# One kernel, two fixed orders: a state-space layer and a long convolution on one core, with the scan's downward pass, the coarse scan and the turning of x cut differently

## The chip, the cores and the metric

The kernel runs on one core of one Trainium2 chip. The metric is device time in microseconds (us) of one execution; lower is better. Five engines work side by side, each through its own instructions in the order in which they were written: TensorE (PE: matmuls, with weight loads as PEld), VectorE (DVE), ScalarE (ACT), GpSimd (POOL) and SyncE (SP). SP, ACT and POOL also issue DMAs. An instruction starts when all before it on its engine have started or ended as the engine demands, and when the semaphores that it waits for are up.

## The reference

Two heads over a sequence of 2048 steps and 640 channels, all in bf16, side by side in the output.

Head A is a diagonal state-space layer with 640 complex states:

```
dt = exp(log_dt);  Lam_bar = exp(dt * Lam)
B_bar = ((Lam_bar - 1) / Lam)[:, None] * Bmat
Bu = einsum("bld,pd->blp", x, B_bar)
h_t = Lam_bar * h_{t-1} + Bu_t                 # 2048 steps
y = 2 * einsum("blp,dp->bld", h, Cmat).real + x * Dskip
```

Head B is a long convolution by channel, gated:

```
k_shift = four taps of k by shift_k            # causal, per channel
kv = k_shift * v
y = irfft(rfft(pad(kv)) * rfft(pad(ssm_k)))[:2048] + kv * ssm_D
out = q * y
```

## The kernel before

Head A. The 640 complex states stand as ten state tiles j = 0 to 9 of 128 rows (64 real parts, 64 imaginary parts). The 2048 steps are cut in 16 residues modulo 16, in two halves hf of eight; each half has two groups b of four. `dn{b}_{j}_{hf}` (L633, ten matmuls of 512 columns) projects x on tile j, from `xT`, x turned so that channels are rows. The first half of `xT` is made on TensorE: two loads `xn0`, `xn1`, then `px` (L582, transposes against the identity into PSUM) and `ex` (the copies to SBUF, by ACT or DVE). The second half comes by eight DMA transposes `x1..` (L597). B's four quarters `B00`, `B01` (states 0 to 319) and `B10`, `B11` (320 to 639) come by DMA transpose too (L608). Then a scan in three levels: `e1`, `m1`, `e3` go up inside a half; `S`, `eS`, `jw`, `jcw`, `jsw`, `jaw`, `scan` and their `v` twins (a_coarse) scan the 128 coarse steps of a group of tiles in one chain of DVE operations; `d1`, `a1`, `d00` to `a02` (a_down) go down again, matmul by matmul (L721, L738) with a DVE addition after each (L727, L744). `ct` and `ect` build the output matrix, `py{part}_{r}{i}` (L788, L792) projects the states and adds x times Dskip, `ey` copies to SBUF and `st` stores.

Head B works in five blocks G of 128 channels. Its FFT is done by matmuls: `s1` (L912, 32 matmuls) and `s2` (L948, 16) turn the filter (`h`, loaded by `hst`, completed by `dtap`) and the gated input (`k`); `pP`, `pQ`, `pY` multiply spectra on DVE; `i2` (L1004, 16) starts the way back, `zt` (L1011) is a DMA transpose of 1 MB, `i1` (L1040, 64 matmuls) ends it, `ob` multiplies by q and stores. Before it, `cv`, `cs`, `ca`, `cm` do the four taps and the gate, `kvs` writes the block to DRAM and `kvl` loads it in another layout. `e1h`, `e1k`, `e2h`, `e2k`, `e3` followed by two digits are the copies from PSUM (L212 on ACT, L214 on DVE).

What sets the order: `ORDER`, a string of operation names written out by hand or by a search beforehand. `place` walks it and emits each operation on its engine (`/A` ACT, `/D` DVE, `/G` POOL, `/S` SP where there is a choice). So each engine's queue is that string, filtered. `place` also gives out buffers: six of 8 KB a partition, seven of 4 KB, two for `yo`, and four PSUM tiles of two banks that every matmul group of the kernel shares. A group of matmuls waits until the last reader of its PSUM tile is done. SP's queue in the string's order carries nearly all loads, transposes and stores.

In `build` the coarse scan runs for tiles 0 to 3 and then for 4 to 9 (`NF` is 4), and a_down takes tiles in pairs.

Of the kernel before, what the change touches and what calls it, by code (L numbers as in the profile page):

```python
# [9 lines left out]
ALU = mybir.AluOpType  # L10
# [13 lines left out]
NF = 4  # L24
PEC = ()
# [111 lines left out]
ld_ldt ld_lre J0 consts J1 nrow ld_lim zero E0 pidx B00 w0 c4 nrowf ci0 xn1 xn0 par E1 ld_dsk/G B01 p0 dtb bc Dm0 w1 p1 fi w2  # L137
nrho ph mk ci1 px10 rn px12 ex10/D px14 ld_sk/S R px00 v0 wi0 px02 trig kz0/D wm0 ex02/A k0 rc px04 ex12/A ss ex00/A set_2_0/D
set_1_0/G ex14/A Dm1/S set_3_0/D x100 set_8_0/G ex04/A dn1_4_0 x101 set_12_0/G sk Ct dn0_4_0 x110 set_4_0/G cs200/A scol
set_3_1/D hst0/S set_1_1/G x111 dn0_1_0 e1_4_0/A set_2_1/G set_4_1/D dn1_1_0 cv300/A m1_4_0 set_12_1/G dn1_0_0 e1_1_0/D x120  # L140
e3_4_0/A ca200 dn1_2_0 ws0 x121 dn0_3_0 cs100/D ca100 x130 dn0_2_0 cs000/D dn1_3_0 x131 ca000 dn0_0_0 e1_3_0/A k1 cm00 m1_1_0
e1_0_0/A m1_3_0 kvs0/G dtap0/D e1_2_0/D m1_0_0 e3_1_0/A s1h03 e3_3_0/D B10 m1_2_0 s1h01 e1h03/D e1h01/A s1h00 e3_2_0/D
e3_0_0/D s1h02 e1h00/A kz1/D set_8_1/D dn0_3_1 e1h02/D B11 dn0_1_1 cs210/D wi1 s2h01 ct s2h00 dn1_3_1 wm1 dn1_1_1 e2h01/A
cv310/D kz2/G k2 k3 hst1/G e2h00/A dn0_2_1 dn1_2_1 e1_3_1/A e1_1_1/D dn0_0_1 ca210 e1_2_1/A dn1_0_1 cs110/D m1_3_1 ca110
e1_0_1/A m1_1_1 m1_2_1 m1_0_1 e3_3_1/D cs010/A e3_2_1/D dn1_9_0 e3_0_1/D e3_1_1/D S0 den v1 dtap1/G ca010 dn0_9_0 eS0/A jw0
ws1 jcw0 dn1_9_1 jsw0 jaw00 dn0_7_1 scan0 dn0_7_0 jcv0 dn1_7_1 kvl0/S e1_9_0/D V cm10 dn1_7_0 e1_7_1/A m1_9_0 kvs1/G dn0_9_1
e1_7_0/D m1_7_1 e3_9_0/D s2h02 e1_9_1/A g m1_7_0 m1_9_1 e3_7_1/A s1k03 e3_7_0/A e3_9_1/A s1k01 e2h02/D e1k03/A s1k00 s1k02
e1k01/A set_G_0/D s2h03 set_G_1/D e1k02/A jv0 v2 jsv0 e1k00/A jav01 s1h11 jav00 s1h12 e2h03/A e1h11/D d1_0 e1h12/A cv320/D
s1h10 a1_0 s1h13 hst2/S dn0_6_0 e1h13/A e1h10/D d00_0 s2h13 cs220/D s2k02 a00_0 e2h13/A dn1_6_0 e2k02/A s2k03 ca220 d01_0
s2h12 e1_6_0/A e2k03/D dtap2/G e2h12/A m1_6_0 a01_0 s2h11 s2h10 e3_6_0/A e2h11/A d02_0 cs120/D e2h10/A s1h22 a02_0 s1h21 s1h23  # L150
e1h22/A ca120 s1h20 kvl1/S e1h21/A dn0_5_1 e1h20/D cs020/A dn1_5_1 diagD dn1_5_0 ca020 e1h23/A s2k00 s2k01 e2k00/D dn0_5_0
e2k01/A s1k12 cn00 cn10 cm20 s1k13 e1k12/A kvs2/S e1_5_1/D s1k11 e1k13/A e1_5_0/D m1_5_1 s1k10 e1k11/A e3_5_1/D m1_5_0 kz3/D
e1k10/A dn0_4_1 s2k10 pP00 pQ00 e3_5_0/A cs230/A s2k11 pP01 dn1_6_1 pQ01 e2k11/A dn1_4_1 e2k10/A dn0_6_1 pY01 dn0_8_1 e1_4_1/A
pY00 e1_6_1/A i202 cn01 cn11 dn1_8_1 e302/A pP10 hst4/S m1_6_1 i201 pQ10 e3_6_1/A m1_4_1 i203 e301/A pY10 q0/S i200 e3_4_1/A
dn0_8_0 e300/A e303/D kvl2/S dn1_8_0 e1_8_1/D ct00 e1_8_0/A m1_8_1 cv330/D dtap4/G ct01 m1_8_0 e3_8_1/A ect00/D ct10 ect01/A
e3_8_0/D ct11 ct20 ect10/A S4 ca230 ect20/A ect11/A ct21 eS4/D ct30 ct31 ect21/A jw4 jcw4 ect31/A d1_1 jsw4 ect30/A ct40
ect40/A jaw40 ct41 zt0 s1k23 scan4 ect41/A s1k20 s1k21 e1k23/A s1k22 e1k21/A jcv4 e1k22/A jv4 a1_1 e1k20/A jsv4 d00_1 s2k20
jav41 cs130/A s2k21 jav40 e2k20/D d1_4 e2k21/A d1_3 a1_4 d1_2 a1_3 i101 a1_2 i210 ob01 i211 e310/A v3 e311/A py0_33 a00_1
ca130 d00_3 d00_2 d00_4 a00_3 py1_33 a00_4 py0_31 ey_33/A a00_2 st_33/S py1_31 cs030/D ca030 s2k13 s2k12 ey_31/A d01_2 cm30
e2k13/A st_31/S py0_00 e2k12/A kvs3/S a01_2 d01_3 pP11 s2k23 s2k22 e2k23/A pQ11 py1_00 e2k22/A pY11 py0_30 kvl3/S ey_00/A  # L160
a01_3 hst3/G st_00/S i213 i212 e313/A k4 d02_3 py1_30 e312/A kz4/D a02_3 d01_1 s1k33 ey_30/A a01_1 s2h22 s1h42 e1k33/A s2h23
e2h22/D s2h21 e2h23/A dtap3/G e1h42/D s2h20 st_30/S e2h21/A s1k30 e2h20/D s1k31 s1k32 e1k30/A pP20 e1k32/A py0_01 pQ20 e1k31/A
py1_01 pY20 d01_4 d02_1 ey_01/A d02_2 a01_4 cv340/A st_01/S s1h40 s1h41 a02_2 e1h40/A s1h43 a02_1 e1h41/A d02_4 cs240/D i100
e1h43/A ca240 py0_32 cs140/A a02_4 s2h42 py1_32 ob00 e2h42/A ca140 s1h30 ob0/S s1h31 ey_32/A cs040/D s1h32 e1h30/A st_32/S
s1h33 ca040 e1h31/A py0_22 e1h32/A py1_22 e1h33/A pP21 v4 q2/S s2k30 pQ21 s2k31 ey_22/A e2k30/A s2h43 st_22/S py0_11 pY21
e2k31/A s2h31 e2h43/A cm40 s2h30 e2h31/A py1_11 kvs4/S e2h30/A s2h40 s2h41 ey_11/D e2h40/A i222 st_11/G i221 e322/A py0_10
e321/D e2h41/A kvl4/G s2h32 i220 e2h32/D i223 q4/G e320/A py1_10 e323/A s2k32 pP30 s2k33 ey_10/A pQ30 s2h33 e2k33/A st_10/S
py0_21 pY30 e2h33/A s1k41 zt2 s1k43 e1k41/A e2k32/D py1_21 e1k43/A s1k40 ey_21/A s1k42 e1k40/A py0_20 st_21/G e1k42/A py1_20
s2k40 pP31 pQ31 q3/S pY31 s2k41 ey_20/A e2k40/D e2k41/A st_20/S zt1 i231 py0_12 pP40 e331/A i230 s2k42 pQ40 e330/A s2k43
py1_12 e2k43/A pY40 e2k42/A i232 i233 pP41 i120 e332/A q1/S e333/A pQ41 py0_23 ey_12/A pY41 py1_23 st_12/S zt3 ob20 i110  # L170
ey_23/A i240 ob10 i242 i241 e342/A i243 e340/D e341/A i121 st_23/S e343/A py0_03 ob21 zt4 ob2/G py1_03 i130 ey_03/A i131
st_03/G ob30 py0_13 ob31 py1_13 ob3/S i111 ey_13/A i141 st_13/S ob11 i140 ob41 ob1/S py0_02 ob40 py1_02 ob4/S ey_02/A st_02/S
# [3 lines left out]
class Kernel:  # L176
# [386 lines left out]
    def a_loads(self):  # L563
# [4 lines left out]
        for b in range(2):  # L568
# [3 lines left out]
            for k in (0, 2, 4):  # L572
                w = min(2, 5 - k)
                pt = self.g.buf("P", f"px{b}{k}")

                def f(e, k=k, w=w, pt=pt, xa=xa):
                    for kk in range(w):
                        for r in range(2):
                            for q in range(2):
                                c = 128 * (5 * (2 * q + r) + k + kk)  # L580
                                o = 512 * kk + 256 * r + 128 * q
                                nc.tensor.matmul(self.P(pt)[:, 0, :].bitcast(bf16)[:, o:o + 128], lhsT=self.S8(xa)[:, c:c + 128],  # L582
                                                 rhs=self.ident[:], start=True, stop=True, is_transpose=True)
                op(f"px{b}{k}", {"PE": mm_cost(128, 4 * w)}, f, r=[f"xn{b}", "ident"], w=[f"px{b}{k}"], bufs=[pt, xa],
                   due=self.DUE["x0"] + 0.5 * k + 3.0 * b)
                op(f"ex{b}{k}", {"ACT": act_c(512 * w), "DVE": dve_tt(512 * w)}, lambda e, b=b, k=k, w=w, pt=pt: self.copy(
                    e, self.xT[:, k:k + w, 0, 2 * b:2 * b + 2, :].rearrange("p k r m -> p k (r m)"),
                    self.P(pt)[:, 0, :].bitcast(bf16)[:, 0:512 * w].rearrange("p (k n) -> p k n", k=w)),
                   r=[f"px{b}{k}"], a=[f"x0{b}"], bufs=[pt], port=False)
# [22 lines left out]
    def a_up(self):  # L612
# [3 lines left out]
        self.Sb = self.cw[2]  # L616
# [30 lines left out]
    def a_coarse(self, js, due):  # L647
# [6 lines left out]
        t1, t2, vv = (self.cw[i] for i in range(3))  # L654
        ps = self.g.buf("P", f"pS{nm}")

        def fS(e):
            P = self.P(ps)[:].rearrange("p a n -> p (a n)")
            for i, j in enumerate(js):
                for c, (lt, q) in enumerate(((self.ident, 4), (self.M[4][:, j, :], 3), (self.M[8][:, j, :], 2), (self.M[12][:, j, :], 1))):  # L660
                    nc.tensor.matmul(P[:, 128 * i:128 * i + 128], lhsT=lt[:] if c == 0 else lt, rhs=self.Qb[:, j, q, :],
                                     start=(c == 0), stop=(c == 3))
        op(f"S{nm}", {"PE": mm_cost(128, 4 * n)}, fS, r=[f"q_{j}" for j in js] + [f"M_{m}_{h}" for m in (4, 8, 12) for h in sorted({j // 5 for j in js})] + ["ident"],
           w=[f"pS{nm}"], bufs=[ps], due=due)
        self.evac(f"eS{nm}", N, lambda: flat(self.Sb[:, 0:n, :]), lambda: self.P(ps)[:].rearrange("p a n -> p (a n)")[:, 0:N],
                  r=[f"pS{nm}"], w=["cw3"], bufs=[ps])
        sk = ["cw3"]
# [38 lines left out]
    def a_down(self, j0, due):  # L706

# [3 lines left out]
        js = (j0, j0 + 1)  # L711
        hs = sorted({j // 5 for j in js})
        nm = j0 // 2
        pt = self.g.buf("P", f"pd{nm}")

        def f1(e):
            P = self.P(pt)
            for i, j in enumerate(js):
                rhs = self.Qb[:, j].rearrange("p q n -> p (q n)")
                for n, w in ((4, 384), (8, 256), (12, 128)):  # L720
                    nc.tensor.matmul(P[:, i, 384 - w:384], lhsT=M[n][:, j, :], rhs=rhs[:, 0:w], start=(n == 4), stop=(n == 12))  # L721
        op(f"d1_{nm}", {"PE": mm_cost(768, 2)}, f1, r=[f"Q0_{j}" for j in js] + [f"q_{j}" for j in js] + ["Qz"] + [f"M_{n}_{h}" for n in (4, 8, 12) for h in hs],
           w=[f"pd{nm}"], bufs=[pt], due=due)

        def f2(e):
            o = self.Qb[:, j0:j0 + 2, 1:4, :].rearrange("p j q n -> p j (q n)")
            v.tensor_tensor(out=o, in0=self.P(pt)[:, :, 0:384], in1=o, op=ALU.add)  # L727
# [450 lines left out]
```

## Time and profile before

| | |
|---|---|
| median of three runs | 225.51 us (225.41 to 225.54) |
| profiled execution: its time | 225.54 us |
| profiled execution: span, first to last instruction | 223.7 us |
| PE busy | 191.3 us, 86%, 3942 matmuls |
| DVE busy | 176.6 us, 79%, 255 instructions |
| ACT busy | 143.5 us, 64%, 164 instructions |
| POOL busy | 30.2 us, 14% |
| DMA | 33.72 MB in 100454 packets, mean 151 GB/s |
| granted TensorE clock, mean | 0.988 |

The busy shares are averages. A matmul's recorded time runs on into the next one's, since matmuls are pipelined: 240 matmuls of L788 show 300 ns each, yet ten in a row take 1.47 us. So PE's work is better read from the distance between the starts of matmul groups. On DVE and ACT too a recorded time overlaps the next one a little: three copies of 1220 ns on DVE in a row take 3.48 us.

### The profile page before, as it was taken

Reading aid. Unit: us, or ns where it says so; the run is one execution under the profiler, and the core shown is the slowest. Engines: PE = TensorE matmul, PEld = TensorE weight load, DVE = VectorE, ACT = ScalarE, POOL = GpSimd, SP = SyncE. Lnnn points to the kernel's source line nnn. Section 1 sums busy time; section 2 is a strip of 40 time slices with the busy share of each in tenths; the row PEclk is TensorE's granted clock in tenths of the full one; section 3 lists DMA queues with packets and bytes.
Section 4 is the critical chain, followed back from the end, with each engine's and each line's share of the span. In section 5 each row is a group of like instructions: output and inputs, shape, how many; then the busy total and the mean of one; then the engine's idle time right before and its main releaser. Section 6 shows DMA issues by size and latency. Waiting matters only on the chain. (4 is left out here: it accounts for less than half of the span.)

```text
span 223.7 us, 8667 instructions
## 1 busy us (share of the span) xinstructions
PE 191.3 (86%) x3942; PEld 135.2 (60%) x3945; DVE 176.6 (79%) x255; ACT 143.5 (64%) x164; POOL 30.2 (14%) x41
## 2 busy tenths in 40 slices
PE   0077959999969998899979999989999999977792
PEld 0064536555555575555657776857878877875581
DVE  7589997788888799998899996999756948842460
ACT  3946935867385798687893176878887768561011
POOL 6619904000100000000000002000005010002100
PEclk9999996999999999999999999999999999999998
DMA  4998859974997059099192348700993999999576
GB/s 87 239 162 121 177 122 224 230 163 97 245 179 146 3 115 221 15 229 193 26 170 34 95 148 195 126 32 3 171 264 84 214 247 160 215 208 198 138 180 156
DMA packets 100454, 33.72 MB, mean 151 GB/s; under 512 B 96866, under 2 KB 98530, under 8 KB 100418
## 3 DMA queue, kind: packets, MB, share of 16 engines
q1 hardware_dynamic: 99204, 29.02, 67.8%
q0 software_dynamic: 1184, 4.16, 6.9%
q8 instruction: 30, 0.49, 1.0%
q14 instruction: 6, 0.05, 0.1%
q10 hardware_dynamic: 30, 0.00, 0.0%
HBM read 9.19 MB, written 7.86 MB: 76 GB/s over the span
## 5 line engine op out<-in xcount | busy, mean ns | idle before, releaser
L212 ACT CAST s<-ps 128x1024 bf16<-128x1024 f32 x82 | 78.9, 1022 | 23.4 <-PE ps L1004 8.2
L633 PE MATMUL ps<-xT,BC 128*64 128x512 bf16 x400 | 46.9, 381 | 2.1 <-ACT xT L212 0.9
L788 PE MATMUL ps<-BC,hb 128*128 128x320 bf16 x240 | 36.5, 300 | 0.0
L633 PEld LDWEIGHTS <-BC 128*64 128x64 bf16 x400 | 22.1, 110 | 21.3 <-issue 4.2
L212 ACT CAST yo<-ps 128x640 bf16<-128x640 f32 x15 | 10.4, 693 | 29.8 <-PE ps L792 23.0
L788 PEld LDWEIGHTS <-hb 128*128 128x128 bf16 x240 | 21.7, 98 | 11.8 <-issue 3.0
L912 PE MATMUL ps<-R,s 64*64 64x128 bf16 x1280 | 23.5, 224 | 6.1 <-DVE s L813 2.2
L214 DVE CAST s<-ps 128x1024 bf16<-128x1024 f32 x18 | 21.8, 1220 | 8.1 <-PE ps L948 4.2
L971 DVE TENSOR_TENSOR s<-s,s 128x2048 bf16<-128x2048 bf16 x20 | 24.4, 1223 | 3.1 <-DMA out_dram<-s 1.3
L912 PEld LDWEIGHTS <-s 64*64 64x64 bf16 x1280 | 20.2, 111 | 11.0 <-issue 8.0
L948 PE MATMUL ps<-s,Wre 128*64 128x128 bf16 x320 | 21.2, 222 | 0.8 <-ACT s L212 0.5
L1047 DVE TENSOR_TENSOR s<-ps,s 128x1024 bf16<-128x1024 f32 x10 | 12.0, 1221 | 12.4 <-PE ps L1040 12.4
L948 PE MATMUL ps<-s,Wim 128*64 128x128 bf16 x320 | 20.8, 219 | 0.0
L948 PEld LDWEIGHTS <-Wre 128*64 128x64 bf16 x320 | 17.9, 109 | 4.2 <-issue 2.2
L744 DVE TENSOR_TENSOR hb<-ps,hb 128x1024 bf16<-128x1024 f32 x15 | 18.0, 1220 | 2.1 <-PE ps L738 2.1
L879 ACT ACTIVATE s<-s,sk 128x2048 bf16<-128x2048 bf16 x8 | 16.1, 2016 | 4.6 <-DVE s L971 2.1
L887 DVE TENSOR_TENSOR s<-s,s 128x2048 bf16<-128x2048 bf16 x15 | 18.5, 1233 | 0.4
L948 PEld LDWEIGHTS <-Wim 128*64 128x64 bf16 x320 | 18.2, 110 | 0.3
L1040 PE MATMUL ps<-Ct,s 128*64 128x64 bf16 x640 | 11.8, 196 | 4.4 <-issue 4.3
L212 ACT CAST hb<-ps 128x768 bf16<-128x768 f32 x12 | 9.5, 800 | 9.2 <-PE ps L633 9.2
L971 DVE TENSOR_TENSOR s<-s 128x1024 bf16<-128x1024 bf16 x20 | 13.7, 688 | 0.3
L397 POOL TENSOR_TENSOR M<-E,ss 128x640 bf16<-128x640 bf16 x7 | 12.1, 1756 | 5.7 <-DVE ss L387 5.7
(159 smaller groups left out, 268.1 us busy)
## 6 DMA issues: line engine op xcount, KB each, us to landing
out_dram<-yo SPq DMA_DIRECT2D x13, 160.0 KB, 3.6
s<-kvd SPq DMA_DIRECT2D x4, 512.0 KB, 4.2
s<-in_B_q_dram SPq DMA_DIRECT2D x4, 512.0 KB, 5.3
out_dram<-s SPq DMA_DIRECT2D x4, 512.0 KB, 4.1
s<-in_B_ssm_k_dram SPq DMA_DIRECT2D x3, 512.0 KB, 5.0
kvd<-s SPq DMA_DIRECT2D x3, 512.0 KB, 3.4
s<-in_A_x_dram SPq DMA_DIRECT2D x2, 640.0 KB, 8.1
kvd<-s POOLq DMA_DIRECT2D x2, 512.0 KB, 5.7
```

Source lines behind the costliest of these rows:

```text
L212: self.nc.scalar.copy(out=out, in_=in_)
L214: self.eng[e].tensor_copy(out=out, in_=in_)
L397: self.eng[e].tensor_tensor(out=mt[:, js, :].rearrange("p j (r i) -> p j r i", r=2), in0=E[:].rearrange("p (a b i) -> p a b i", a=1, b=1). ...
L633: nc.tensor.matmul(P[64 * ri:64 * ri + 64, b, :], lhsT=self.BT[:, k, ri, 64 * j:64 * j + 64], rhs=self.xT[:, k, hf, 2 * b:2 * b + 2, :].re ...
L744: v.tensor_tensor(out=o, in0=self.P(p2)[:].rearrange("p j (h m) -> p j h m", h=2), in1=o, op=ALU.add)
L788: nc.tensor.matmul(P[:, part, 0:320], lhsT=hap(j), rhs=self.CT[:, j, c0:c0 + 320], start=(j == 0), stop=False)
L879: nc.scalar.activation(out=out, in_=k(j), func=ACT.Copy, scale=self.sk[:, G, j:j + 1])
L887: op(f"ca{j}{G}{h}", {"DVE": dve_tt(W_)}, lambda e, c=c, tt=tt: v.tensor_tensor(out=c(), in0=c(), in1=tt(), op=ALU.add), r=[f"tm{G}{h}"], ...
L912: nc.tensor.matmul(P[64 * ri:64 * ri + 64, r, 128 * b4:128 * b4 + 128], lhsT=d[64 * r:64 * r + 64, 4 * qd + b4, a0, :], rhs=self.R[64 * r: ...
L948: nc.tensor.matmul(P[64 * pi:64 * pi + 64, ri, 128 * k4:128 * k4 + 128], lhsT=W[:, kp, pi, :], rhs=A[:, kp + 16 * pi, :], start=True, stop ...
L971: v.tensor_tensor(out=o, in0=a, in1=b, op=op_)
L1047: v.tensor_tensor(out=o, in0=self.P(pt)[:].rearrange("p s (b a c) -> p a (s b) c", b=8, a=16), in1=o, op=ALU.mult)
```

## The change

`ORDER` is replaced by another string, and three parts of the work are cut differently; the arithmetic of the result is the same.

- x is turned with plain matmuls into f32 PSUM, one bank for each k (before: transposing matmuls into 16-bit PSUM, two k in one bank), and the copies `ex` read f32.
- a_down takes one tile at a time: ten `a1` of 384 columns and thirty `a0` of 512, each with matmuls of its own, in place of five `a1` of 768 and fifteen `a0` of 1024.
- The coarse scan runs for tiles 0 to 4 and 5 to 9, and its first copy `Sb` has a buffer of its own.

The string moves work between engines. ACT takes ten of the twenty scalings `cv`/`cs` (before eight), 13 of the unit copies `e1` (12), 12 of `e3` (10), 13 of `ey` (15); DVE takes the others. POOL builds eight of the twelve matrices `set` (before seven of twelve; two more, `set_G`, are on DVE in both). The head and the tail of the string, old and new:

```diff
 ORDER = """
-ld_ldt ld_lre J0 consts J1 nrow ld_lim zero E0 pidx B00 w0 c4 nrowf ci0 xn1 xn0 par E1 ld_dsk/G B01 p0 dtb bc Dm0 w1 p1 fi w2
-nrho ph mk ci1 px10 rn px12 ex10/D px14 ld_sk/S R px00 v0 wi0 px02 trig kz0/D wm0 ex02/A k0 rc px04 ex12/A ss ex00/A set_2_0/D
-set_1_0/G ex14/A Dm1/S set_3_0/D x100 set_8_0/G ex04/A dn1_4_0 x101 set_12_0/G sk Ct dn0_4_0 x110 set_4_0/G cs200/A scol
-set_3_1/D hst0/S set_1_1/G x111 dn0_1_0 e1_4_0/A set_2_1/G set_4_1/D dn1_1_0 cv300/A m1_4_0 set_12_1/G dn1_0_0 e1_1_0/D x120
-e3_4_0/A ca200 dn1_2_0 ws0 x121 dn0_3_0 cs100/D ca100 x130 dn0_2_0 cs000/D dn1_3_0 x131 ca000 dn0_0_0 e1_3_0/A k1 cm00 m1_1_0
-e1_0_0/A m1_3_0 kvs0/G dtap0/D e1_2_0/D m1_0_0 e3_1_0/A s1h03 e3_3_0/D B10 m1_2_0 s1h01 e1h03/D e1h01/A s1h00 e3_2_0/D
-e3_0_0/D s1h02 e1h00/A kz1/D set_8_1/D dn0_3_1 e1h02/D B11 dn0_1_1 cs210/D wi1 s2h01 ct s2h00 dn1_3_1 wm1 dn1_1_1 e2h01/A
...
-py1_12 e2k43/A pY40 e2k42/A i232 i233 pP41 i120 e332/A q1/S e333/A pQ41 py0_23 ey_12/A pY41 py1_23 st_12/S zt3 ob20 i110
-ey_23/A i240 ob10 i242 i241 e342/A i243 e340/D e341/A i121 st_23/S e343/A py0_03 ob21 zt4 ob2/G py1_03 i130 ey_03/A i131
-st_03/G ob30 py0_13 ob31 py1_13 ob3/S i111 ey_13/A i141 st_13/S ob11 i140 ob41 ob1/S py0_02 ob40 py1_02 ob4/S ey_02/A st_02/S
+xn1 ld_lre J0 consts nrow xn0 J1 zero ld_ldt E0 pidx w0 ld_lim c4 nrowf hst1/G B00 E1 kz0/G wi0 bc Dm0 px12 Dm1/G w1 px10
+ex12/A px14 ex10/A wm0 px00 w2 par px02 p0 ex00/D B01 px04 ex14/D dtb mk k0 R ex02/A p1 fi dtap1/G ex04/A s1h13 nrho ph rn Ct
+s1h10 ld_sk/S scol B10 e1h13/D s1h11 trig den dn1_4_0 e1h11/A rc B11 ss e1h10/A dn0_4_0 set_3_0/D set_1_0/G x100 dn0_1_0
+set_2_0/G e1_4_0/D x101 dn0_2_0 sk cs200/D set_8_0/G m1_4_0 v0 cv300/A dn1_2_0 kz1/G set_12_0/D set_3_1/G e3_4_0/A dn0_7_0
+e1_2_0/A set_1_1/G dn1_3_0 ca200 x110 set_2_1/G dn0_3_0 x111 cs100/A dn1_1_0 set_4_1/G x120 m1_2_0 set_4_0/D dn1_7_0 set_8_1/G
+x121 e1_1_0/A e1_3_0/A m1_1_0 ca100 x130 m1_3_0 e3_1_0/A dn0_0_0 e3_2_0/A e1_7_0/D cs000/A x131 dn1_0_0 set_12_1/D k1 g
+e3_3_0/A m1_7_0 s1h12 e1_0_0/A dn1_9_0 e1h12/A ca000 m1_0_0 dn0_9_0 ld_dsk/S cm00 dn1_6_0 e1_9_0/A kvs0/S e3_0_0/D dn0_0_1
+e3_7_0/D set_G_1/D dn1_0_1 set_G_0/D diagD dn0_1_1 dn1_1_1 e1_0_1/D kvl0/S hst0/S ws0 cs210/A wi1 m1_0_1 e1_1_1/D dn0_6_0 wm1
+m1_1_1 m1_9_0 e3_9_0/A ws1 v1 dn1_4_1 e3_1_1/D e3_0_1/D e1_6_0/D s1k03 s1k00 e1k03/D dn0_4_1 e1k00/D s1k01 dtap0/G V e1_4_1/A
...
+i232 st_23/S e333/A i230 pP41 i231 e332/A py0_33 pQ41 e330/A py1_33 pY41 e331/A zt3 py0_31 pP40 ey_33/A i243 pQ40 i242 e343/A
+py1_31 pY40 e342/A i241 ey_31/A st_33/S i240 e341/D i120 st_31/S e340/A i121 ob20 zt4 ob21 py0_11 i131 ob2/S py1_11 ob31 i130
+ey_11/A py0_22 st_11/S ob30 i141 ob3/S i140 ob41 py1_22 ob40 py0_20 ey_22/D ob4/S st_22/S py1_20 ey_20/A st_20/S
 """
...
-                                nc.tensor.matmul(self.P(pt)[:, 0, :].bitcast(bf16)[:, o:o + 128], lhsT=self.S8(xa)[:, c:c + 128],
-                                                 rhs=self.ident[:], start=True, stop=True, is_transpose=True)
+                                nc.tensor.matmul(self.P(pt)[:, kk, 256 * r + 128 * q:256 * r + 128 * q + 128], lhsT=self.S8(xa)[:, c:c + 128],
+                                                 rhs=self.ident[:], start=True, stop=True)
...
-        self.Sb = self.cw[2]
+        self.Sb = T([128, 5, 128], bf16, "Sb")
...
-    def a_down(self, j0, due):
+    def a_down(self, j, due):
...
+            rhs = self.Qb[:, j].rearrange("p q n -> p (q n)")
+            for n, w in ((4, 384), (8, 256), (12, 128)):
+                nc.tensor.matmul(P[:, 0, 384 - w:384], lhsT=M[n][:, j, :], rhs=rhs[:, 0:w], start=(n == 4), stop=(n == 12))
...
+            v.tensor_tensor(out=o, in0=self.P(pt)[:, 0, 0:384], in1=o, op=ALU.add)
...
+                src = self.Qb[:, j, 0:4, :].rearrange("p (h q) n -> p h (q n)", h=2) if r == 0 else hv(r - 1)
+                nc.tensor.matmul(self.P(p2)[:, 0, :].rearrange("p (h m) -> p h m", h=2), lhsT=M[1][:, j, :], rhs=src, start=True, stop=True)
...
+                v.tensor_tensor(out=hv(r), in0=self.P(p2)[:, 0, :].rearrange("p (h m) -> p h m", h=2), in1=hv(r), op=ALU.add)
...
-        self.a_coarse(list(range(NF)), U["c0"])
-        for j in range(0, NF, 2):
+        self.a_coarse(list(range(5)), U["c0"])
+        for j in range(5):
             self.a_down(j, U["d0"] + U["d1"] * j)
-        self.a_coarse(list(range(NF, 10)), U["c1"])
-        for j in range(NF, 10, 2):
-            self.a_down(j, U["e0"] + U["e1"] * (j - NF))
+        self.a_coarse(list(range(5, 10)), U["c1"])
+        for j in range(5, 10):
+            self.a_down(j, U["e0"] + U["e1"] * (j - 5))
```

## The prediction

> **What bounds the kernel now.** I read the totals first, then three long stretches of the span, then waits and groups, then the chain and the DMA queues. The stretches (busy us and, in brackets, instructions of PE, PEld, DVE, ACT, POOL) are cut where the string's work is comparable later on:
>
> ```profile
> span 223.7 us, 8667 instructions
> 0.00:48.80 48.80, 32.49 (x412) 20.73 (x414) 41.11 (x84) 31.51 (x39) 22.30 (x30) 0.97 0.92 175
> 48.80:148.60 99.80, 93.03 (x1872) 61.70 (x1874) 89.21 (x128) 69.41 (x81) 2.70 (x5) 1.00 0.64 125
> 148.60:223.70 75.10, 65.77 (x1665) 52.81 (x1664) 46.30 (x45) 42.62 (x46) 5.20 (x6) 0.99 0.81 169
> ```
>
> The reader is to see three regimes. Until 48.8 DMA is 92% busy and PE a third idle: loads set the pace. From 48.8 to 148.6 PE and DVE are both near full and neither alone is the bound. After 148.6 DVE has air and PE has none. The chain of waits says the same: from 150.5 on it is PE alone, matmul group after matmul group, but for two holes in which PE waits for nothing that the profile shows ("issue"):
>
> ```profile
> 198.90 1.17 PE ps L1040 x63
> 200.07 2.82 issue
> 202.89 0.19 PE ps L1040
> ...
> 206.19 1.73 PE ps L1040 x101
> 207.91 1.45 issue
> 209.36 0.60 PE ps L1040 x27
> ```
>
> Both holes lie inside one `i1` group, whose 64 matmuls have no wait between them. The DMA queues name a candidate:
>
> ```profile
> q8 instruction: 30, 0.49, 1.0%
> ```
>
> 30 packets of 16 KB for some 7,890 weight loads and matmuls are one packet for about 260 of them. Each hole ends 1.3 to 1.5 us after such a packet, and the two are 256 PE instructions apart. Where PE passes 256 instructions in normal time, they take 4.4 us and more; the ones ahead of these holes add up to 3.3 and 4.7 us of work, while a `zt` transpose of 1 MB fills the DMA engines. An inference, then: PE runs out of instructions.
>
> The other rows that the sum uses, as groups by shape and as waits:
>
> ```profile
> L744 DVE TENSOR_TENSOR hb<-ps,hb 128x1024 bf16<-128x1024 f32 x15 | 18.0, 1220 | 2.1 <-PE ps L738 2.1
> L727 DVE TENSOR_TENSOR Qb<-ps,Qb 128x768 bf16<-128x768 f32 x5 | 4.7, 952 | 0.7 <-PE ps L721 0.7
> L214 DVE CAST Qb<-ps 128x256 bf16<-128x256 f32 x10 | 3.9, 419 | 1.5 <-PE ps L641 1.5
> L683 DVE TENSOR_TENSOR cw<-sinT,ps 128x512 bf16<-128x512 bf16 x2 | 1.4, 688 | 1.5 <-PE ps L679 1.5
> L214 DVE COPY xT<-ps 128x1024 bf16<-128x1024 bf16 x1 | 0.7, 691 | 2.7 <-PE ps L582 2.7
> L397 POOL TENSOR_TENSOR M<-E,ss 128x640 bf16<-128x640 bf16 x7 | 12.1, 1756 | 5.7 <-DVE ss L387 5.7
> 34.23 2.63 SPq L608 DMA_TRANSPOSE BC<-in_A_B_re_dram  x1
> 36.91 3.10 SPq L608 DMA_TRANSPOSE BC<-in_A_B_im_dram  x1
> ```
>
> The last column of a group is DVE's idle time before it: fifteen paired additions L744 waited 2.1 us for PE together, 0.14 each.
>
> **The change part by part: the loads of the engines.** Downward pass on DVE: removed 15 x 1.220 + 5 x 0.952 = 23.1; added 30 x 0.688 (the row of 512 columns from PSUM) + 10 x 0.55 (between the rows of 256 and 512 columns) = 26.1, so +3.0. The copies of x on DVE: one of 0.691 becomes one of 1.220 and one of 0.688, +1.2. Changed choice of engine for copies, scalings and `set`: DVE -3.2, ACT +4.2 less 0.7 for x. Sum: DVE +1, ACT +3.5, PE unchanged but for two short `jw`, `jv` matmuls. No engine's total is a reason for a change of the time; the order is.
>
> I therefore added up, along both strings, each engine's durations ahead of given operations: on PE the usual distance between group starts (`dn` 1.1, `m1` 0.33, `s1` and `s2` 0.51, `i2` 0.5, `i1` 1.13, `py` 1.55), on DVE and ACT the rows' means. They are sums of queued work, not times. Before: when `dn1_9_0` starts at 48.76, PE has 28.6 us of work behind it, DVE 43.5, ACT 35.8; when `s1h40` starts at 148.59, 120.0, 138.7 and 110.4. After, ahead of `dn0_6_0`: 28.0, 39.0, 32.1; ahead of `d02_2`: 120.0, 134.6, 117.9.
>
> **First stage, to PE's 28 us of work: -3.4.** Before, PE is 20.1 us behind its work at its end. After:
> - `xn1`, `xn0` are issued at 0.74 and not at 3.11. They took 7.6 and 8.7 us to land, so `px` starts near 8.5 (before 10.74). But the small parameters now come later: `par` stands behind `px00`, so p0 is near 11 instead of 3.5; from there the DVE queue (ex00 1.2, ex14 0.7, mk and R 1.7, p1, fi, nrho 1.3), then rn 1.7 and trig 0.8 on ACT, rc and ss 1.3, give `ss` at 19.9 (before 15.7). Two `set` on POOL at 1.76 follow: `m1_4_0` near 23.5 (before 21.2), with 8.7 us of work ahead of it (before 7.1). So PE is 14.8 behind its work there, before 14.1: a small loss.
> - `B10`, `B11` (2.63 + 3.10 of SP) now stand ahead of all `x1`, with `k0` (2.9) and `ld_sk` (0.6) between. From B01's issue, which ended at 10.1 before and may end at 11.5 with `hst1`'s 0.5 MB on POOL's queue beside, B11 is issued out at 19 to 21 and lands 5.2 later (its row), at 24.5 to 26.5. `dn0_7_0` needs it near 25: at most 1.5 of wait.
> - That buys work of the first half for tiles 7, 9 and 6 while the `x1` transposes run. Before, PE had none left at 30.1 and stood 3 us. The eight `x1` (1.28 each when not held up), `v0` and the two B put the last issue at 33 to 37.5 and the landing, 1.7 to 3.3 later, at 35 to 41. `dn0_0_1` has 23.3 of work ahead: it starts at 38.2 at the earliest (14.9 behind), at 41 at the latest by these rows. I take 39.5, nearer the later bound since DMA was 92% busy, and 0.5 for copies: 16.7 behind, against 20.1.
>
> **Second stage, from 28 to 120: +1.6.** Before it took 99.8 us for 91.4 of PE and 95.2 of DVE. After: 92.0 and 95.6; I take the mean of the two additions, +0.5. ACT has 85.8 where it had 74.6; it stays below DVE, cost 0 as long as its two long blocks (`ws1` after `cs210`, `ct` of 4 us) lie where DVE empties PSUM, which the string does there. PE changes between kinds of group 92 times against 81; a change costs 0.13 (`s2` to `s2` 0.42, `s2` to `py` 0.57): 1.4, of which I take 0.5 since DVE shares the bound; ends 0 and 1.4. `kvl0` waits for `cm00` (near 38), `kvs0` (3.4 to 6.2 to land) and itself 4.2: 46.5 to 49 for `s1k03` wanted near 48: 0.6 taken, ends 0 and 2.5, `hst0` for `s1h02` behind it on SP included. The hand-overs from PE to DVE double to forty: a pair waited 0.14 on the mean, and the string puts other tiles' work between the steps of one tile, so I take 0 for the twenty more; ends -2 (the pairs' own 2.1 + 0.7 nearly gone) and +2.8 (twenty at 0.14).
>
> **Third stage, PE's last 64.5: +0.4.** PE work 64.7 against 64.5, changes 40 in both. For the instruction holes I added PE's work between every 256th instruction: near the end the new string has 4.28 and 3.59 with `zt3` and `zt4` under way; if each is stretched to the 6.2 us of the two stretched ones of before, that is 4.5 against 4.27. `zt4` (landing 7.2 to 8.5 after issue) has 9 us of other PE work between its last source `i240` and `i141`. Last copy and store are the same.
>
> The Trainium skill, page "Runtime: NRT & Kernel Launch", section "Instruction fetch mechanics", says that instructions come in 16 KiB blocks of 256 and that crossing a block is mostly hidden. The 2.82 and 1.45 us rows above speak against "hidden" here; by the page no string would lose time to fetch, the third stage's term would be 0 and the sum 223.7 us.
>
> **Sum.** 223.7 - 3.4 + 1.6 + 0.4 = 222.3 span. The profiled execution took 225.54 with 1.84 around its span, 0.03 above the median; so 224.1 us, 0.6% faster. A difference under about 0.2% (0.45 us) can't be told from none in this kernel.
>
> **Rivals.**
> - *Slower: the transposes are late.* One queue carries xn, B, k0, v0 and `x1`. If the last `x1` lands at 44 instead of 39.5 (hst1's 0.5 MB at 150 GB/s is 3.5 us more), PE stands as long: 228.6. It decides from a landing near 41. For it: DMA 92% busy. Against: the bytes ahead are the same but for hst1.
> - *Slower: single updates hand over badly.* Twenty more hand-overs through four PSUM tiles. At 0.14 each 226.9; at 0.5, the mean of the four that did wait for L738, 234. It decides from 0.07. Against: up to eight tiles are interleaved.
> - *Faster by more: no holes near the end.* The new tail puts a `py` group between nearly all `i1` groups. Without fetch holes 4.7 falls away: 219.4. Against: the sums of 3.59 and 4.28.
> - *No change:* the first stage's gain is returned in the second.
>
> **How the numbers follow.** Forecast, faster by 0.2 to 2%: 0.34. More than that: 0.16. Within 0.2%: 0.08. Late transposes: 0.20. Hand-overs: 0.22. So faster 0.50, same 0.08, slower 0.42. The range leaves out 1 in 10 at each end: from a little under the hole-free case, 217.5, to past the late transposes, 230.5. The forecast's own range is 221 to 225.
>
> **What the profile after would show.** First stage: `dn0_0_1` at 38 to 41, `ss` near 20, little PE wait between. Second: about 100 us from `dn0_6_0` to `d02_2`, a_down's additions on DVE idle little before they start. Third: issue holes of 4 to 5 us inside `i1` after `zt3`. Wrong if the first half's units wait for B11 beyond 27, if `s1k03` waits for `kvl0` by more than 3, or if DVE idles over 10 us in the second stage.

## The result, and the profile after

The changed kernel takes 218.79 us (median of 4 runs, 218.27 to 220.55) where before takes 225.52 (225.41 to 225.90). The ratio is 0.971, 95% interval 0.966 to 0.977: 2.9% faster. The forecast was 224.1 us and 0.6%, the range 217.5 to 230.5. On the two other chips that both kernels ran on, the ratio is 0.984 (0.977 to 0.991; before 223.64) and 0.974 (0.968 to 0.981; before 224.39). On the second of them four of six runs, 220.6 to 221.6 us, lie over 1.5% above the fastest and are not in the ratio; the median of all six, 220.9 us, is 0.984 of before. Single runs of the new kernel lie up to 4.3 us apart on one chip; part of that is explained below.

Here are the span of the profiled run (218.27 us in all) and the three stretches, cut at the same amounts of PE work as in the prediction (at `dn0_6_0` and `d02_2`). Columns as before: from and to, length, busy us and instructions of PE, PEld, DVE, ACT, POOL, then granted clock, DMA share, GB/s.

```profile
span 215.9 us, 8689 instructions
0.00:41.49 41.49, 32.27 (x382) 19.15 (x382) 36.51 (x95) 29.15 (x36) 20.71 (x29) 0.96 0.89 170
41.49:145.56 104.07, 97.30 (x2064) 66.06 (x2063) 91.28 (x124) 79.75 (x91) 7.94 (x10) 0.99 0.77 154
145.56:215.90 70.34, 65.42 (x1506) 51.61 (x1502) 49.77 (x51) 37.99 (x41) 2.58 (x3) 0.99 0.73 152
```

| stage | before | after | difference | predicted |
|---|---|---|---|---|
| first, to 28 us of PE work | 48.80 | 41.49 | -7.3 | -3.4 |
| second, to 120 | 99.80 | 104.07 | +4.3 | +1.6 |
| third | 75.10 | 70.34 | -4.8 | +0.4 |
| span | 223.7 | 215.9 | -7.8 | -1.4 |

The sum hides three larger misses: two stages gained more than forecast, one lost more. In the third stage the holes in which PE waited for nothing are gone. The chain of waits there is PE without a break, but for one copy on ACT and one wait for the transpose `zt4`:

```profile
191.31 1.00 PE ps L973 x32
...
193.91 1.02 PE ps L973 x32
194.95 1.02 ACT s L212
195.99 9.15 DMA s<-s
205.18 2.21 PE ps L1009 x128
```

The last line but one is `zt4`, 9.15 us from its issue until `i141` (L1009, the last line) starts; PE itself stood 1.0 us for it. The instruction queue moved as much as before. The groups that the prediction counted, with DVE's idle time in the last column:

```profile
q8 instruction: 30, 0.49, 1.0%
L735 DVE TENSOR_TENSOR hb<-ps,hb 128x512 bf16<-128x512 f32 x30 | 19.2, 684 | 5.6 <-PE ps L731 5.6
L721 DVE TENSOR_TENSOR Qb<-ps,Qb 128x384 bf16<-128x384 f32 x10 | 5.1, 551 | 0.1
L214 DVE CAST Qb<-ps 128x256 bf16<-128x256 f32 x8 | 3.2, 419 | 1.2 <-ACT s L212 0.7 <-PE ps L638 0.5
L397 POOL TENSOR_TENSOR M<-E,ss 128x640 bf16<-128x640 bf16 x8 | 14.5, 1845 | 3.9 <-DVE ss L387 3.9
14.32 1.55 SPq L605 DMA_TRANSPOSE BC<-in_A_B_re_dram  x1
15.91 2.98 SPq L605 DMA_TRANSPOSE BC<-in_A_B_im_dram  x1
```

The single additions cost what was forecast (0.684 and 0.551 us each), and DVE stood 5.6 us in front of them where it stood 2.1 in front of the pairs. `B10` and `B11` were issued by 18.9 us, earlier than the 19 to 21 reckoned with.

In the first stage `xn1` landed sooner than reckoned; the chain's line:

```profile
0.74 4.89 DMA s<-in_A_x_dram
```

In the second stage one wait is new. First the waits of the form that `dtap3` and `hst3` make, as totals of the whole run (us, times, longest; of the two on `PEld`, PE's weight loads, the one of 3.6 is that of `s1h13` at the start), then the rows around `s1h33`:

```profile
POOL s L803 <- DMA s<-in_B_ssm_k_dram: 12.6, 3, 6.4
PEld L881 <- POOL s L803: 5.7, 2, 3.6
```

```profile
140.20 0.24 PE L973 MATMUL ps<-s,Vim 64*128 64x128 bf16 x2
142.02 0.26 POOL L803 TENSOR_TENSOR s<-s,Dm 128x16 bf16<-128x16 bf16 x1 [6.37 <-DMA s<-in_B_ssm_k_dram]
142.33 3.30 PE L881 MATMUL ps<-R,s 64*64 64x128 bf16 x128 [1.90 <-POOL s L803]
```

`s1h33` (L881) waits for `dtap3` on POOL, and that for the load `hst3`, which POOL issued at 132.95 and which landed at 141.94. The last product ahead of it starts at 140.2, `s1h33` at 142.33: PE lost 2.1 us, 1.90 of it idle by the row. The expectations of `tap_later` and `half_tap` below say 2.7; that counts from 139.6, where `i221` starts, whose 16 products PE was still working on.

### The profile page after: what moved, and what is told of

Same layout as the page of the kernel before. It is cut to its first block, busy times and chain, and to the rows that moved or that the text cites. A ratio compares the mean times of both kernels' runs of the same rounds, so it can differ in the third digit from the quotient of the medians.

```text
span 215.9 us, 8689 instructions
## 1 busy us (share of the span) xinstructions
PE 195.0 (90%) x3947; PEld 136.8 (63%) x3947; DVE 177.6 (82%) x269; ACT 146.9 (68%) x166; POOL 31.2 (14%) x42
## 4 chain that ended last, share of the span: by engine, by line
PE 72%; ACT 7%; DVE 7%; DMA 7%; issue 4%; POOL 2%; ACTq 0%; POOLq 0%
PE ps L630 19%; PE ps L778 18%; PE ps L881 10%; PE ps L917 8%; DMA s<-s 4%; PE ps L973 4%; PE ps L1009 3%; PE ps L638 3%; ACT s L212 3%; DMA s<-in_A_x_dram 2%; DVE hb L735 2%; PE ps L782 2%; PE ps L715 2%; PE ps L731 2%; POOL M L397 1%
## 5 line engine op out<-in xcount | busy, mean ns | idle before, releaser
L630 PE MATMUL ps<-xT,BC 128*64 128x512 bf16 x400 | 46.4, 381 | 0.5 <-ACT Qb L212 0.5
L881 PE MATMUL ps<-R,s 64*64 64x128 bf16 x1280 | 25.0, 232 | 5.9 <-DVE Fi L337 3.5
L212 ACT CAST yo<-ps 128x640 bf16<-128x640 f32 x13 | 9.0, 691 | 28.5 <-PE ps L782 27.4
L881 PEld LDWEIGHTS <-s 64*64 64x64 bf16 x1280 | 21.4, 116 | 10.8 <-POOL s L803 5.7
L940 DVE TENSOR_TENSOR s<-s,s 128x2048 bf16<-128x2048 bf16 x20 | 24.4, 1221 | 0.7 <-ACT s L212 0.2
L735 DVE TENSOR_TENSOR hb<-ps,hb 128x512 bf16<-128x512 f32 x30 | 19.2, 684 | 5.6 <-PE ps L731 5.6
L848 ACT ACTIVATE s<-s,sk 128x2048 bf16<-128x2048 bf16 x10 | 20.0, 2013 | 3.7 <-DVE s L856 2.1
L917 PEld LDWEIGHTS <-Wre 128*64 128x64 bf16 x320 | 17.9, 109 | 4.7 <-issue 3.4
L856 DVE TENSOR_TENSOR s<-s,s 128x2048 bf16<-128x2048 bf16 x15 | 20.1, 1338 | 0.5 <-ACT s L848 0.3
L397 POOL TENSOR_TENSOR M<-E,ss 128x640 bf16<-128x640 bf16 x8 | 14.5, 1845 | 3.9 <-DVE ss L387 3.9
L212 ACT CAST hb<-ps 128x768 bf16<-128x768 f32 x13 | 10.3, 799 | 3.9 <-PE ps L630 3.8
L1009 PE MATMUL ps<-Ct,s 128*64 128x64 bf16 x640 | 11.5, 196 | 1.6 <-DMA s<-s 1.0
```

Of the source, the lines that this page charges most:

```text
L212: self.nc.scalar.copy(out=out, in_=in_)
L397: self.eng[e].tensor_tensor(out=mt[:, js, :].rearrange("p j (r i) -> p j r i", r=2), in0=E[:].rearrange("p (a b i) -> p a b i", a=1, b=1). ...
L630: nc.tensor.matmul(P[64 * ri:64 * ri + 64, b, :], lhsT=self.BT[:, k, ri, 64 * j:64 * j + 64], rhs=self.xT[:, k, hf, 2 * b:2 * b + 2, :].re ...
L735: v.tensor_tensor(out=hv(r), in0=self.P(p2)[:, 0, :].rearrange("p (h m) -> p h m", h=2), in1=hv(r), op=ALU.add)
L848: nc.scalar.activation(out=out, in_=k(j), func=ACT.Copy, scale=self.sk[:, G, j:j + 1])
L856: op(f"ca{j}{G}{h}", {"DVE": dve_tt(W_)}, lambda e, c=c, tt=tt: v.tensor_tensor(out=c(), in0=c(), in1=tt(), op=ALU.add), r=[f"tm{G}{h}"], ...
```

## The experiments

They ran in three sets, each on a chip of its own beside runs of before, which took 223.41, 223.64 and 224.39 us there. So ratios to before are compared, and times within a trace. In the second and third set the new kernel ran once more, unchanged.

**Are the holes at instruction numbers?** Before, with idle products put in where PE is idle anyway:

```diff
         op("par", {"PE": 0.1}, f_par, r=["praw", "ident"], w=["par"], bufs=[self.par], due=-25)
+        pad = self.g.buf("P", "pad")
+
+        def f_pad(e):
+            for c in range(64):
+                nc.tensor.matmul(self.P(pad)[:, 0, 0:10], lhsT=self.ident[:], rhs=self.ident[:, 0:10], start=True, stop=True)
+        op("pad", {"PE": 0.1}, f_pad, r=["ident"], w=["pad"], bufs=[pad])
```

> The kernel before with 64 idle 10-column products (128 PE instructions, weight load and matmul each) put on PE behind `par`, in its idle time before `px10` (2.9 to 10.7 us). Nothing else moves, but every 256-instruction boundary now falls 64 matmuls, one `i1` group, earlier in the work. Theory of instruction fetch (PE stands where a piece of 256 instructions holds less work than the fetch of the next one takes, about 3.5 us from boundary to boundary, 6.2 with a `zt` transpose on its way): the holes of 2.82 and 1.45 us inside `i121` and `i131` leave their places, and the ones of 1.57 and 1.2 at `s1h12` and `dn1_6_0` with them; new ones come where the shifted pieces are short, which at 61.4 (2.0 us of work), 76.9 (2.7), 140.4 (3.0) and 195.6 (3.3) they are; the time stays within -1 to +3 us of 225.5. Rival (the holes belong to the `i1` groups or to `zt`, not to instruction numbers): the holes stay at the same matmuls and the time is 225.5.

Measured: 1.016 of before (1.008 to 1.024), 226.2 us against 223.4. The holes inside `i121` and `i131` are gone, and those at `s1h12` and `dn1_6_0`. New ones lie inside `s2h03` (1.0 us), `s1h13` (0.9), `s1k31` (1.2), `py1_20` and `i111`. The last two in the chain of waits:

```profile
179.97 0.14 PE ps L799 x3
180.11 1.44 issue
181.55 1.52 PE ps L795 x10
...
207.58 0.30 PE ps L1047 x11
207.89 2.64 issue
210.53 3.38 PE ps L1047 x128
```

Counted by PE instructions all five stand where the four of before stood: at multiples of 256 behind one another, to within 6. Two of the four pieces named in advance ended in a hole (from 61.4, to `s2h03`, and from 140.4, to `s1k31`); at the ends of those from 76.9 and 195.6, with 2.7 and 3.3 us of work, there was no hole. The two largest holes, in `py1_20` and `i111`, were not named in advance: they end pieces with 4.8 us of work. So the holes do follow the instruction numbers, but a fixed price of 3.5 us for a piece is wrong both ways.

**Does the new order have no holes of itself?** The same 64 products in the new kernel, behind `px04`.

> The kernel after with the same 64 idle products, behind `px04`, where PE is idle from 10.1 to 13.6 us. Theory of instruction fetch: the boundaries leave the places they have now; pieces of 2.1 us (from 167.2) and 2.1 us (from 194.8) come up where PE has no slack, 1.4 us of hole at each, and some 0.9 more elsewhere in the last stage: +2 to +4 us over 218.8. Rival (the change got rid of the holes by putting other work between the `i1` groups): no holes, 218.8 within 0.5.

Measured: 1.008 of before (1.005 to 1.012), where the new kernel unchanged has 0.971 to 0.984 on three other chips: some 5 to 8 us lost with the order untouched. The holes inside groups lie in `s1h00`, `py0_30`, `i121` and `i130`, 1.5, 1.1, 0.8 and 2.5 us from one matmul to the next, each at a multiple of 256. The first and the last:

```profile
52.51 0.49 PE ps L888 x21
53.00 1.26 issue
54.26 0.36 PE ps L888 x11
...
206.27 0.69 PE ps L1016 x36
206.96 2.31 issue
209.28 0.75 PE ps L1016 x28
```

The rival has fallen. What keeps the new kernel free of such holes is where the boundaries lie in its string, not that `py` groups stand between `i1` groups. The loss is larger than forecast, among other things because the piece that ends in `i130` took 7.6 us and not the 6.2 assumed.

**Is the early B the gain of the first stage?** In the new order (the places that the units of tiles 7, 9 and 6 leave are not shown):

```diff
 scol
-B10
 e1h13/D
...
-B11
 ss
...
 x131
+B10 B11
 dn1_0_0
...
 m1_1_1
+dn0_7_0 dn1_7_0 e1_7_0/D m1_7_0 e3_1_1/D e3_0_1/D dn1_9_0 dn0_9_0 dn1_6_0
+e1_9_0/A e3_7_0/D dn0_6_0
 m1_9_0
...
+e1_6_0/D m1_6_0 e3_6_0/D
...
```

> The kernel after with `B10` and `B11` back behind all `x1` transposes, and the units 7, 9 and 6 of the first half, which need them, behind `dn1_1_1`. The prediction's reason for the first stage (work that needs no `x1` fills the time of the `x1` transposes): the fill is gone, but the `x1` are issued 4.5 us earlier, with a last landing near 29.5 where PE reaches `dn0_0_1` at 30.1; so PE still does not wait there, the two units' worth of order is worth nothing by itself, and the first 28 us of PE work end within 1 us of 41.5. Rival (the early B is the gain): PE stands 3 us or more near 30, as before, and the time is 3 to 5 us above 218.8.

Measured: 1.007 of before (1.004 to 1.011), so some 5 to 8 us above the new kernel by its ratios on three other chips. In PE's queue `dn1_4_1`, with 0.3 us more work ahead of it, starts at 52.21 and not at 43.5 to 44.9. PE's waits from 20 to 55 us (total, times, longest):

```profile
PE ps L638 <- DVE hb L214: 4.3, 4, 2.2
PE ps L638 <- ACT hb L212: 2.4, 3, 2.0
```

No wait is for `x1`, as the first theory said: `dn0_0_1` ran at 34.4 without one. But the time is lost all the same, the rival's 3 to 5 us or more: PE waits for copies of its own results, which stand on DVE and ACT behind the first group's convolution, `set_G` and `diagD`. Part of the longest wait is a load's: DVE itself stood 1.5 us in front of `diagD` for Dskip (`ld_dsk`). In the new kernel this window (18 to 50 us) has one wait:

```profile
PE ps L630 <- ACT Qb L212: 0.5, 1, 0.5
```

So the early B is a gain, and as these waits read it, by another mechanism than the prediction's: more tiles in flight give the copies time. The run moves `B10` and `B11` together with the units that need them and can't part the two.

**What was before's hole at 30 us?** In the order of before:

```diff
 cs100/D ca100
+dtap0/D
 x130
...
 kvs0/G
-dtap0/D
 e1_2_0/D
```

> The kernel before with `dtap0`, 0.2 us on DVE, moved up in DVE's queue from behind `cm00` to behind `ca100` (from 32.9 to about 29.7 us; its load landed at 27.9). The prediction took before's hole of 3 us at 30.1 for a want of work while the `x1` transposes run. Theory now (PE's order reaches `s1h03` there, and that waits for `dtap0` in DVE's queue): the wait of 2.2 us at 33.2 is gone, and the time falls by 1 to 2 us. The prediction's reason: PE meets the missing `x1` 2 us earlier instead, no gain.

Measured: 1.000 of before (0.997 to 1.004), no gain. `s1h03` starts at 29.58 and not at 32 to 33, but the next group, `m1_2_0`, then waits 2.45 us. PE's row, and what DVE did meanwhile:

```profile
32.68 0.49 PE L641 MATMUL ps<-hb,M 128*128 128x256 bf16 x3 [2.45 <-DVE hb L214]
```

```profile
28.48 0.75 DVE L881 TENSOR_SCALAR s<-s,sk 128x2048 bf16<-128x2048 bf16 x1
29.27 1.23 DVE L887 TENSOR_TENSOR s<-s,s 128x2048 bf16<-128x2048 bf16 x1
30.53 1.22 DVE L889 TENSOR_TENSOR s<-s,s 128x2048 bf16<-128x2048 bf16 x1
31.68 0.95 DVE L214 CAST hb<-ps 128x768 bf16<-128x768 f32 x1
```

The copy that `m1_2_0` needs (31.68) stands behind 3.2 us of convolution. Theory and rival both had this wrong: neither `dtap0` alone nor `x1` held PE, but DVE's queue.

**The 16-bit transposes of x.** The functions of before's `a_loads` in the new kernel (16-bit PSUM tile, `is_transpose=True`, copies of 16-bit columns); beside it the new kernel unchanged.

> The kernel after, unchanged, beside the runs of before that the next three are measured against: 0.971 of before (0.966 to 0.977) if the gain does not hang on the chip. On the chip of the first four experiments before took 223.4 and not 225.5 us; if after's gain lies in places that differ between chips, the ratio here moves towards 0.98, which is what the variant with the later `dtap3` gave there.

> The kernel after with the 16-bit transposes of x (transposing products into a 16-bit PSUM tile, and copies of 16-bit columns) of before put back; order and engines as in after. The prediction gave this part +1.2 us of DVE and +0.7 of ACT before 16 us, none of it named as bounding. If that is right, the time falls by 0 to 0.7 us. Rival (the copies set the start: `s1h13`, `ss` and with them `m1_4_0` stand behind them on DVE): `m1_4_0` moves from 20.8 to 19.6 and the time falls by 1.2 or more.

Measured: unchanged 0.984 (0.977 to 0.991), with 16 bit 0.990 (0.982 to 0.998). Its runs are 220.6, 220.9, 223.4 and 223.7 us, the unchanged kernel's 219.2 to 222.4. There is no gain, and in the profiled runs `m1_4_0` is later, at 24.3 and not 20.9 us. The reason is not the copies: two of them took 1.01 us on DVE (1.81 from 32 bits) and 1.93 on ACT in both forms. It is a load. The chain of waits of the 16-bit kernel's profiled run (223.4 us), and of the unchanged one:

```profile
5.12 11.11 DMA Dm<-in_B_ssm_D_dram
16.70 2.77 PE ps L884 x79
```

```profile
5.12 7.75 DMA Dm<-in_B_ssm_D_dram
13.44 2.78 PE ps L881 x92
```

`s1h13` waits for `dtap1` on POOL, and that for `Dm1`. Issued at 5.12 in both, it landed at 16.24 and at 12.88, and all that follows is 3.3 us later. From `s1h13` to the end the two traces take 204.3 and 203.9 us. So the 16-bit form is worth nothing either way that these runs can tell.

**What do single hand-overs cost in the old order?** Every `d1_k`, `a1_k`, `d0r_k`, `a0r_k` of before as two single ones, with the new kernel's `a_down`:

```diff
-d1_0
+d1_0 d1_1
...
-a1_0
+a1_0 a1_1
...
-for j in range(0, NF, 2):
+for j in range(NF):
```

> The kernel before with its downward pass one state tile at a time: every product and addition of a pair replaced by two single ones in its place (where no PSUM tile is free, behind the next copy that frees one), the coarse scan still of 4 and 6 tiles. DVE's work rises by 30 x 0.684 - 15 x 1.22 + 10 x 0.55 - 5 x 0.952 = 2.9 us, and hand-overs from PE to DVE double. Theory (the second stage was mis-sized by these hand-overs: after had 5.6 us of DVE idle in front of the single additions, before 2.1): the time rises by 3 to 6 us over before. Rival, the prediction's own 0 for the hand-overs: +1.5 at most, half of DVE's extra work.

Measured: 1.059 of before (1.053 to 1.064), 13 us, twice the theory's upper end. The groups:

```profile
L739 DVE TENSOR_TENSOR hb<-ps,hb 128x512 bf16<-128x512 f32 x30 | 19.2, 684 | 5.1 <-PE ps L735 4.9
L725 DVE TENSOR_TENSOR Qb<-ps,Qb 128x384 bf16<-128x384 f32 x10 | 5.5, 556 | 1.9 <-PE ps L719 1.8
```

Busy time rose by 2.0 and idle time in front by 4.2 over before's rows: 6.2 of the 13. The rest is spread over many short stops of PE around 112 to 147 us, each for an operation of ACT or DVE. The rival (+1.5) has fallen. How much of the 13 us belongs to the singles, and how much to an order never laid out for them, stays open.

**Moving the wait for `hst3`.** `d02_2`, `py0_12` and `py1_12` ahead of `s1h33` in the new order (the copy `ey_12` moves up with them; the places they leave are not shown):

```diff
 a02_8
+d02_2 py0_12
+a02_9 e321/A
+py1_12 a02_2
 s1h33
```

> The kernel after with `d02_2`, `py0_12` and `py1_12` put ahead of `s1h33`, which there waits 2.7 us for `dtap3` and the load `hst3` behind it (landed 141.94). Theory (the hole is PE's alone, and PE sets the end from there on): 2.2 to 2.7 us of the 2.72 are gained, 216.1 to 216.6. Rival (DVE, 0.88 busy in this stage, or the instruction pieces give it back): under 1 us gained.

Measured: 0.980 of before (0.975 to 0.985), 219.3 us, against 0.984 and 0.974 for the unchanged kernel in the other sets: not told apart. From `d02_9` to `s1k31` the trace takes 16.4 us, those of the unchanged kernel 17.0 to 17.2. The wait shrank, but a hole came at the next boundary, where 3.2 us of work were left for the piece:

```profile
149.22 1.01 PE ps L881 x47
150.23 1.14 issue
151.37 0.46 PE ps L881 x17
```

**A better version, in three steps,** with the unchanged kernel beside them. Only `d02_2` and `py0_12` moved (`half_tap`); then `Dm0` and `Dm1` moved ahead of `hst1`; then `py1_22` moved ahead of `i141`:

```diff
 J1
+Dm0
...
+Dm1/G
 hst1/G
...
 py0_22 st_11/S
+py1_22
 ob30 i141
```

> The kernel after, unchanged, as the measure for the three that follow: 0.971 of before on the first chip, 0.984 on the second; a value between these, its runs 219 to 221 us, some 2 to 3 us above where the small load `Dm1` lands late.

> The kernel after with `d02_2` and `py0_12`, but not `py1_12`, put ahead of `s1h33`. With both `py` moved, the wait of 2.7 us for `dtap3` was gone, but the piece of 256 instructions from `s1h32` to `s1k30` was left with 3.2 us of work, and a hole of 1.41 us came at its end. Theory of instruction fetch: here the piece keeps 4.5 us of work, no hole; 1.8 us of the wait are filled: 1.5 to 1.8 us below the unchanged kernel, against about 0.9 with both moved. Rival (the hole at `s1k30` has another cause): it stays, gain under 0.7.

> The last one, and the small load `Dm1` issued ahead of `hst1` on POOL's queue, near 2 us and not at 5.1. `dtap1` and, behind it on POOL, `ph` wait for it; it landed at 12.9 to 13.1 us in the short runs of after, and at 16.2 in the run of 223.4 us of the variant with 16-bit transposes, in which `s1h13` started at 16.7 and not at 13.4. Theory (this landing sets the start of PE's queue, and its spread is the spread of the runs): the runs above 221 us go, median 0 to 0.7 us lower. Rival (the spread is that of all loads in the first 16 us): same median and spread as the last one.

> The last one, and `py1_22` put ahead of `i141`, which waits 1.1 us for the transpose `zt4`. Theory of instruction fetch: the piece fetched while `zt4` is on its way comes 6.2 us after the last boundary whether PE waits for `zt4` or not, so the wait turns into a hole at the boundary: 0 to 0.3 us gained. Rival (the wait alone held PE): 1.1 us gained.

Measured: 0.974 (0.968 to 0.981) unchanged, 0.973 (0.969 to 0.978), 0.991 (0.987 to 0.994) and 0.984 (0.980 to 0.989).

The first step did what fetch theory says: no hole at `s1k30`, and 14.84 us from `d02_9` to `s1k31` (14.84 and 14.92 in the next two steps, which keep this order) where the unchanged kernel took 17.0 to 17.2 in all three of its traces. The times do not settle whether it is a faster kernel: the medians of all six runs are 218.7 and 220.9 us, but both spread too far. Five of its runs took 217.1 to 219.3 us; the profiled one took 221.9, with `Dm1` landing at 16.14.

The second step made it worse. `Dm1` lands no earlier than before, at 12.67 for an issue at 2.52, and `hst1`, now behind it, has become the last to come:

```profile
3.55 11.71 DMA s<-in_B_ssm_k_dram
15.73 2.78 PE ps L881 x84
```

`s1h13` starts at 15.7 in place of 13.4. Both sides were wrong: it is not `Dm1` that sets the start, but whichever of the two loads comes last. Nor is this start the whole of the spread: the profiled run of the unchanged kernel in this set took 221.2 us with `Dm1` landed at 12.83 and `s1h13` started at 13.5.

The third step shows the exchange that was forecast. The wait for `zt4` is gone, and a hole stands at the next boundary, inside `py0_20`:

```profile
209.04 1.46 PE ps L778 x10
210.51 1.71 issue
212.21 0.30 PE ps L782 x3
```

From `i131` to `py1_20` the two traces take 12.13 us without and 12.77 with the third step, as the theory has it. The times lean the other way (0.991 and 0.984, with intervals that overlap), so the exchange is shown and its price is not.

## Why the prediction was right or wrong

The sign and the range held. The sum was 5.3 us too high, 6.4 in the span (the new kernel's median lies 2.9 us above the profiled span, where 1.8 was reckoned), by the terms below. A gain of more than 2% had been given a chance of 0.16. The sign was partly luck: the stage that beat its forecast by most is one where a small loss was forecast, and 64 idle products ahead of it make the same order slower than before (1.008).

- **Third stage, +0.4, measured -4.8: the step that failed.** The prediction stretched the pieces of 4.28 and 3.59 us of work to 6.2 each, because before's two were stretched so: 4.5 us of holes, where none came. Stretching does not follow from `zt3` and `zt4` being about. The pieces took 4.31 and 3.57 us: their packets started 1.1 and 0.7 us after the boundary, those of before 3.7 and 4.1 us after theirs. Before had a sign of this too: its last piece, from 214.2 to 217.7, passed in 3.5 us without a hole, its packet 0.5 us after the boundary, so "4.4 us and more" was not its rule. The one late packet near the end of the new kernel (3.6 us after 199.41) belongs to a piece with 4.9 us of work and the wait for `zt4`: 6.15 us, so nothing is seen of it. The rival "no holes near the end" gave 219.4 and came true, but not for its reason, as the padded kernel shows.
- **The fetch inference itself** was right: the padded kernels moved the holes with the instruction numbers. The Trainium skill, page "Runtime: NRT & Kernel Launch", section "Instruction fetch mechanics", calls a crossing mostly hidden. That fits most boundaries in every trace, but with it one would not look for the 5 to 8 us that the padding cost.
- **First stage, -3.4, measured -7.3: right in sign, mis-sized at the start.** `xn1` and `xn0` took 4.9 and 6.1 us to land, not 7.6 and 8.7; `ss` ended at 17.9, not 19.9; `m1_4_0` started at 20.77, not 23.5. That is 2.7 of the 3.9 us. From there PE fell back 1.4 us, where 1.9 was forecast; 0.6 more is the cut, 28.0 us of work against 28.6. The reason given for before's loss, no work while `x1` is transposed, was wrong: PE waited for `dtap0`, and with that moved up for a copy, both behind the convolution on DVE. The rival "late transposes" did not come about; the last `x1` was issued by 32.1 us and `dn0_0_1` ran at 36.4.
- **Second stage, +1.6, measured +4.3: a term was missing.** The prediction looked at `kvl0` and `hst0`, which cost nothing (`kvl0` landed at 44.12, `s1k03` started at 45.19). It did not look at `hst3`, which the new string issues 7.3 us ahead of PE's need while it takes 9.0 to land: 2.1 us of wait, all of which the version with `d02_2` and `py0_12` moved won back in the trace. What is left, 2.2 us, is near 1.6, but that does not show the other terms right. Two holes of before in this stage, inside `s1h12` and `dn1_6_0`, are gone as well, and the prediction had no term for them; their rows:

```profile
67.23 0.36 PE L912 MATMUL ps<-R,s 64*64 64x128 bf16 x11 [1.30 <-issue]
73.15 1.05 PE L633 MATMUL ps<-xT,BC 128*64 128x512 bf16 x7 [0.60 <-issue]
```

So the loss elsewhere may be larger by up to 1.9 us. The hand-overs were taken at 0, between -2 and +2.8: idle time in front of the additions rose by 2.9 us (5.7 against 2.8), in a stage where PE was the fuller engine (busy 97.3 of 104.07 us, DVE 91.3). DVE idled 12.8 us, over the 10 that the prediction gave as a sign of being wrong, but it had idled 10.6 before. How much of the rest is theirs stays open; the run with singles in the old order shows that 0 depends on the order.

- **The copies of x, +1.2 on DVE and 0.7 less on ACT, on no path:** both sizes held (by the rows' means DVE 0.69 before and 1.90 after, ACT 4.31 and 3.61), and no loss was seen. The expectation of `px16` gives ACT +0.7, which is not what the prediction said; the form of the copies makes 0.80 us on DVE and nothing on ACT.

## What to carry to other kernels

Number the instructions of a PE-bound string in 256s and add up the work in each piece: a piece with little work can end in a hole, it does so where its packet comes late, and every instruction added or taken away ahead of it moves all boundaries, so that a local gain can return as a hole further on. Ask of each hole in a profile which queue held the releaser, before a price is put on its going; moving one small wait often uncovers the next in the same queue. For every load that a new order moves, set its issue, its queue and its earliest reader side by side, not only for those at the stage's edge.

## What the runs showed of the hardware

- **Instruction pieces.** In 13 of the profiles I set the boundaries of 256 PE instructions against the packets of the instruction queue. Of 20 pauses of 0.6 us or more at a boundary, 19 ended 2.2 to 2.8 us after the start of a packet, and one 3.3 us after. The packet started 0.4 to 5.2 us after the boundary ahead. Examples, as boundary, packet, end of the pause: 196.72, 200.48, 203.01 and 203.01, 207.11, 209.36 in before; 169.44, 169.90, 172.48 and 201.71, 205.96, 209.28 in the padded new kernel. The shortest piece without a pause took 2.9 us, with its packet 0.2 us after the boundary. So a piece is late when its packet is late; what holds the packet back is not shown. The boundaries ahead of the two late ones of before lie 2.3 us after the issue of a `zt` transpose, but in the new kernel one lies 2.4 us after such an issue (191.53 after 189.14) and its packet came after 1.1 us.
- **A load with two landing times.** `Dm1`, issued at 5.12 us, landed at 12.80 to 13.15 us in six profiles and at 16.14 and 16.24 in two, and the start of PE's main work moved with it by 3.2 us. The short and the long runs of these two kernels lie about as far apart; that the landing makes this difference in each of them is argued, since only one run of each has a profile. What decides the landing was not tried, but the traces show a companion: in the two late ones SP's issue of the transpose `B01` starts 0.04 and 0.1 us after that of `Dm1`, in the six others 0.2 to 0.7 us after, and `Dm1` lands 0.2 to 1.1 us ahead of `B01` in all eight. In the two profiles with `Dm1` issued at 2.52 us the transpose `B00` starts 0.05 and 0.06 us behind it, and `Dm1` took 10.2 us.
